# One ordered load queue for a spectral and MLP block: loads moved to SP in a fixed sequence, the output fill behind the last filter load, a new instruction order

## The chip, the core and the metric

The kernel runs on one core of a Trainium2 chip. Times are device microseconds of one launch; smaller is better. The kernel before took 172.88 us as the median of three runs (172.51 to 174.43).

The engines are named as the profile names them: PE (TensorE, matrix products), DVE (VectorE), ACT (ScalarE), POOL (GpSimd) and SP (SyncE, which here only issues DMAs). Names with q are an engine's own queue of issues (SPq, POOLq).

## The reference

With x of 2048 rows and 640 columns, bf16:

```python
xn = _layernorm(x, axis=-1)
return x + _A_ref(xn, A_w_r, A_w_i) + _B_ref(xn, B_w1, B_b1, B_w2, B_b2)
```

`_A_ref` is a 2-D real Fourier transform over rows and columns, a pointwise product with the complex filter `w_r + 1j * w_i` (2048 x 321), and the inverse transform. `_B_ref` is a two-layer perceptron, 640 to 1536 to 640, with the tanh form of gelu between the layers.

## The kernel before

The 2048 rows are cut into 16 chunks of 128; chunk c holds the rows p * 16 + c. Everything stays in on-chip memory between the stages.

- **Normalization and folding (DVE, lines 482 to 542).** Each chunk of x gives statistics (L482, L484), a reciprocal root on POOL (`rstd`, L492), and the normalized chunk `xn` (L510). Chunks go in eight pairs; a pair's columns are folded twice (L538, `xe`; L542, `xf`). `xn` has two slots (`p_xn`), so the third pair has to wait until all readers of the first are done.
- **Transposes of xn.** The perceptron needs `xn` with columns on the partitions (`xnT`). Chunks 0 to 5 are transposed on PE (`tps`, L526) and copied out by ACT or DVE; chunks 6 to 15 (`BYDMA`) by a DMA transpose that SP issues (L517), which reads the `xn` slot.
- **First layer (`hps`).** Row blocks hps0 to hps5 cover chunks 0, 1, 2-3, 4-7, 8-11 and 12-15. Each has 12 column tiles of five matmuls, and ACT applies gelu to each tile (L576, `gT`). hps3 needs xnT4 to xnT7, hps4 needs xnT8 to xnT11.
- **Second layer.** For eight chunks (`KEEP`: 1, 2, 4, 5, 7, 8, 10, 11) it is done early (`kps`, four parts of six matmuls) and DVE puts the sum with b2 aside (L736). It needs W2. For the others it stands at the end (`fps`).
- **Transform.** `aps` is the first transform over rows (table G), one per pair, copied into `XV`; `bps` is the transform over columns (table E), which needs all eight pairs; `cps` finishes the rows (table M); DVE multiplies with the filter (L643, needs every filter load) and adds (L647); `dps` (table N) starts the way back; its results `U` go through 16 DMA transposes (L668) into `XV`; `eps` (table GE) and the last product with table H inside `fps` finish it.
- **Output.** Four DMAs first copy x into the output (`B_pre`, L465, the fill); 14 chunks are then added onto it by accumulating DMAs from POOL (L752), each waiting for its part of the fill; chunks 14 and 15 (`DIRECT`) already hold x and are stored from SP (L749).

All matmuls are recorded on one line (L379) and all loads on one (L374); tiles tell them apart. In the profile `W` stands for W1 or W2 and `X`, `gtab`, `T`, `Wf` for the buffers of that name.

The order is written by hand. Operations are numbered as the program creates them; `ORDER` lists number, engine letter (s SP, p PE, a ACT, d DVE, g POOL) and slots, and each engine runs its own entries in that sequence. Waits are worked out from it. Before the change the loads of x, W1, G, the identity and the filter are on SP; W2 (four pieces), b2 and the tables E, M, N, GE, H are on POOL, as is the fill, which waits for nothing. SP's order before begins x0, x1, a filter load, W1 first part, identity, x2, x4, b1, two filter loads, W1 third part, x6, W1 second part; it goes on with x14, G, x10 and x12 among filter loads; then xnT6 and xnT7, thirteen filter loads, xnT11, xnT10, a filter load, x8 (chunks 8 and 9), and the other transposes among filter loads.

The filter comes in 34 loads of up to 80 KB, made of rows of 642 bytes:

```python
load(bass.AP(tensor=Wf, offset=p0 * WP + off, ap=[[2 * WP, 16], [2 * KP, n], [1, 321]]),
     bass.AP(tensor=wsrc.tensor, offset=wsrc.offset + row * 321, ap=[[128 * 321, 16], [step * 321, n], [1, 321]]),
     B_w, 16 * 642 * n, after=[wpad], rate=250e3, issue=0.645, group="W", prio=next(pr))
```

Of the kernel before, what the change touches and what calls it, by code (L numbers as in the profile page):

```python
# [13 lines left out]
D = 640  # L14
F = 1536
# [263 lines left out]


# [16 lines left out]
def bass_parallel_sum__spectral_gfnet__dense_activation_gelu__prompt_kernel(  # L297
# [12 lines left out]
    const = {k: nc.inline_tensor(_bf16_bits(v.reshape(128, -1)), name=f"c_{k}").ap().bitcast(BF) for k, v in T.items()}  # L310
    xv = A_x[0].rearrange("(p c) d -> p c d", c=16)
    ov = out[0].rearrange("(p c) d -> p c d", c=16)
    w1v = B_w1.rearrange("(c p) f -> p c f", p=128)
    w2v = B_w2.rearrange("(c p) e -> p c e", p=128)
    b1v = B_b1.rearrange("(c p) -> c p", p=128)
    b2v = B_b2.rearrange("(o e) -> o e", o=1)

    K = Sched(nc, ["sp", "pe", "act", "dve", "pool"])
    with ExitStack() as es:
# [29 lines left out]
        W2 = sb("W2", [128, NFC, D])  # L349
# [20 lines left out]
        p_xn, p_x1, p_xf, p_xb, p_y, p_t, p_z, p_u = Pool(2), Pool(1), Pool(2), Pool(2), Pool(2), Pool(2), Pool(2), Pool(3)  # L370
        p_yo, p_y2, p_yf, p_os = Pool(2), Pool(1), Pool(2), Pool(8)

        def load(dst, src, buf, nbytes, after=(), reads=(), rate=400e3, q="sp", prio=400, issue=0.45, late=0.0, group=None):
            return K.op([(q, 1.0 if q == "pool" else issue)], prio, lambda e, _: e.dma_start(dst, src), reads=reads, writes=[buf], after=after, dma=(nbytes, rate), late=late, group=group)  # L374
# [38 lines left out]
        B_w = Buf("W")  # L413
# [27 lines left out]
        load(mtab[:], const["M"], B_m, 65536, rate=200e3, q="pool", prio=next(pr2), late=10.0)
        load(ntab[:], const["N"], B_n, 49152, rate=200e3, q="pool", prio=next(pr2), late=10.0)
        load(getab[:], const["GE"], B_ge, 204800, q="pool", prio=next(pr2), late=10.0)
        load(htab[:].rearrange("p a b -> p (a b)"), const["H"], B_h, 524288, q="pool", prio=next(pr2), late=10.0)
# [6 lines left out]
        for ri, wsrc in enumerate((A_w_r, A_w_i)):  # L451
            for pp in range(2):
                for qq in range(2):
                    for lo in range(2):
# [40 lines left out]
        for pair in range(8):  # L495
# [290 lines left out]
```

## Time and profile before

| | |
|---|---|
| Profiled execution, its own time | 174.47 us |
| Span, first to last instruction | 172.7 us |
| Median of the three runs | 172.88 us |
| PE busy | 147.8 us (86%) |
| DVE busy | 111.8 us (65%) |
| ACT busy | 76.0 us (44%) |
| POOL busy | 27.4 us (16%) |
| Mean granted TensorE clock | 0.951 |
| DMA moved | 20.71 MB, mean 120 GB/s |

The page cuts the span into 40 equal slices and gives each engine's busy share in tenths. A line of the stretches gives, after the length, the busy time and the number of instructions of PE, PEld (weight loads, beside PE), DVE, ACT and POOL, then the granted clock, the busy share of the DMA engines, and GB/s. A line of the waits names who waited for whom, the total, how often, and the longest. The chain that ended last and the timelines give start, duration and what ran; an issue on SPq or POOLq is the time that the queue spends on issuing, not the transfer.

### The profile page before, as it was taken

What the parts mean: (1) busy time and instruction counts of PE and PEld (TensorE: products, weight loads), DVE (VectorE), ACT (ScalarE), POOL (GpSimd) and SP (SyncE); (2) the same over time, 40 slices, a digit from 0 to 9 for tenths busy, and PEclk for the clock granted to TensorE, in tenths of its full rate; (3) what the DMA queues carried; (4) which work ended last, traced back from release to release, by engine and by line L of the source; (5) the groups of instructions that cost most, each with busy time, mean ns of one, the idle gap of its engine ahead of it and who ended that gap; (6) DMA issues with size and microseconds to landing.
All of it is one profiled execution on the core that took longest, in us unless ns stands there. A gap on an engine that the chain in (4) does not pass through costs nothing.

```text
span 172.7 us, 4031 instructions
## 1 busy us (share of the span) xinstructions
PE 147.8 (86%) x1702; PEld 90.7 (53%) x1720; DVE 111.8 (65%) x240; ACT 76.0 (44%) x131; POOL 27.4 (16%) x44
## 2 busy tenths in 40 slices
PE   7631989995980099999999999999899999999994
PEld 7531878862630056645445534445455756575563
DVE  2680389998201981279729848888323999998732
ACT  2450677932670046667736786974321322021000
POOL 1610164153000100000000000000000018333520
PEclk9997599999999558999999999999999999999999
DMA  4999999999999550000002500962843036686392
GB/s 113 295 343 305 311 274 254 211 63 237 400 269 213 120 124 9 4 0 4 0 4 45 110 3 4 98 58 60 96 86 70 0 42 71 88 107 80 38 114 78
DMA packets 29705, 20.71 MB, mean 120 GB/s; under 512 B 19160, under 2 KB 27480, under 8 KB 29688
## 3 DMA queue, kind: packets, MB, share of 16 engines
q1 hardware_dynamic: 26264, 12.37, 36.8%
q0 software_dynamic: 3424, 8.10, 21.9%
q8 instruction: 13, 0.21, 0.5%
q14 instruction: 4, 0.03, 0.1%
HBM read 13.58 MB, written 5.24 MB: 109 GB/s over the span
## 4 chain that ended last, share of the span: by engine, by line
PE 53%; DMA 19%; DVE 14%; SPq 8%; issue 3%; ACT 1%; DVEq 0%
PE ps L379 53%; DMA W<-in_B_w_dram 9%; DMA xnT<-T 6%; SPq L517 4%; SPq L374 4%; DMA XV<-U 2%; DVE stats L482 2%; DMA X<-in_A_x_dram 2%; DVE T L510 2%; DVE W L745 2%; DVE Wf L699 2%; DVE Wf L391 1%; DVE Wf L704 1%; DVE T L542 1%; DVE T L538 1%
## 5 line engine op out<-in xcount | busy, mean ns | idle before, releaser
L379 PE MATMUL ps<-xnT,W 128*128 128x512 bf16 (+2 forms) x360 | 63.2, 326 | 9.1 <-DMA W<-in_B_w_dram 6.7
L379 PE MATMUL ps<-W,gT 128*128 128x128 bf16 (+3 forms) x378 | 54.9, 291 | 1.4 <-issue 0.3
L576 ACT ACTIVATE gT<-ps,b1col 128x512 bf16<-128x512 f32 (+2 forms) x72 | 36.9, 546 | 21.8 <-PE ps L379 21.1
L379 PEld LDWEIGHTS ps<-xnT,W 128*128 128x128 bf16 x360 | 30.4, 105 | 30.4 <-issue 10.6
L379 PEld LDWEIGHTS ps<-W,gT 128*128 128x128 bf16 x396 | 30.7, 98 | 23.2 <-issue 0.8
L752 POOL DMA_DIRECT2D out_dram<-W x14 | 12.1, 901 | 94.6 <-DVE W L745 94.6
L482 DVE BATCH_NORM_STATS2 stats<-X 128x6 f32<-128x320 bf16 x32 | 14.1, 479 | 19.8 <-DMA X<-in_A_x_dram 19.8
L390 ACT ACTIVATE XV<-ps 128x1280 bf16<-128x1280 f32 (+1 forms) x8 | 9.5, 1185 | 16.1 <-PE ps L379 16.1
L379 PE MATMUL ps<-gtab,T 128*128 128x128 bf16 x80 | 7.2, 242 | 9.1 <-DVE T L542 9.1
L390 ACT ACTIVATE Wf<-ps 128x960 bf16<-128x960 f32 (+1 forms) x6 | 5.3, 882 | 21.5 <-PE ps L379 21.5
L492 POOL TENSOR_TENSOR rstd<-ve,mhalf 128x2 f32<-128x2 f32 (+1 forms) x8 | 6.0, 759 | 43.5 <-DVE ve L491 43.5
L643 DVE TENSOR_TENSOR T<-Y,Wf 128x1288 bf16<-128x1288 bf16 x16 | 12.7, 823 | 0.0
L379 PEld LDWEIGHTS ps<-gtab,T 128*128 128x128 bf16 x80 | 6.0, 110 | 11.3 <-DVE T L542 9.9
L391 DVE CAST Y<-ps 128x644 bf16<-128x644 f32 x7 | 5.8, 827 | 9.0 <-PE ps L379 9.0
L390 ACT ACTIVATE Xb<-ps 128x960 bf16<-128x960 f32 (+1 forms) x7 | 7.6, 1099 | 5.7 <-PE ps L379 5.7
L542 DVE TENSOR_TENSOR T<-T 128x512 bf16<-128x512 bf16 (+1 forms) x32 | 9.0, 316 | 1.3 <-PE ps L379 1.2
L736 DVE TENSOR_TENSOR X<-ps,b2bc 128x640 f32<-128x640 f32 x7 | 5.7, 820 | 5.5 <-PE ps L379 5.5
L391 DVE CAST Xb<-ps 128x960 bf16<-128x960 f32 (+1 forms) x5 | 5.9, 1174 | 3.6 <-PE ps L379 3.6
L390 ACT ACTIVATE Y<-ps 128x644 bf16<-128x644 f32 x9 | 6.2, 705 | 3.4 <-PE ps L379 3.4
L379 PE MATMUL ps<-getab,XV 32*128 32x160 bf16 (+1 forms) x128 | 7.6, 242 | 0.0
L510 DVE TENSOR_SCALAR T<-X,mv,rstd 128x640 bf16<-128x640 bf16 x16 | 7.0, 456 | 0.7 <-DMA xnT<-T 0.7
L538 DVE TENSOR_TENSOR T<-T 128x640 bf16<-128x640 bf16 x16 | 7.3, 480 | 0.1
(58 smaller groups left out, 131.7 us busy)
## 6 DMA issues: line engine op xcount, KB each, us to landing
out_dram<-in_A_x_dram POOLq DMA_DIRECT2D x4, 640.0 KB, 9.6
X<-in_A_x_dram SPq DMA_DIRECT2D x7, 320.0 KB, 13.1
out_dram<-W POOLq DMA_DIRECT2D x14, 160.0 KB, 3.5
W<-in_B_w_dram POOLq DMA_DIRECT2D x4, 480.0 KB, 9.1
Wf<-in_A_w_r_dram SPq DMA_DIRECT2D x15, 80.2 KB, 8.4
Wf<-in_A_w_i_dram SPq DMA_DIRECT2D x15, 80.2 KB, 8.0
W<-in_B_w_dram SPq DMA_DIRECT2D x1, 800.0 KB, 10.0
W<-in_B_w_dram SPq DMA_DIRECT2D x1, 640.0 KB, 14.8
```

The lines of the kernel that those rows point to most:

```text
L374: return K.op([(q, 1.0 if q == "pool" else issue)], prio, lambda e, _: e.dma_start(dst, src), reads=reads, writes=[buf], after=after, dma= ...
L379: ins = e.matmul(o_, lhsT=lw, rhs=rh, start=st, stop=sp_, skip_group_check=True)
L390: return e.activation(dst(), src(), ACT.Copy, scale=scale)
L391: return e.tensor_copy(dst(), src())
L482: st_ops.append(K.op([("dve", 0.393)], pr, lambda e, _, c=c, h=h: e.bn_stats(stats[:, c, 6 * h:6 * h + 6], view(X, c * D + H2 * h, [[1, H2 ...
L510: o = K.op([("dve", 0.356)], pr, lambda e, _, c=c, n=n, xnv=xnv: e.tensor_scalar(out=xnv(n, 0, [[1, D]]), in0=view(X, c * D, [[1, D]]), sc ...
L517: ring_ops.append(K.op([("sp", 1.28)], 1500, lambda e, _, c=c, n=n, xnv=xnv: e.dma_start_transpose(xnT[:, c, :, :], xnv(n, 0, [[1, D]])), ...
L538: K.op([("dve", 0.39)], pr, lambda e, _, k=k, op=op, xnv=xnv, x1v=x1v: e.tensor_tensor(out=x1v(H2 * k, [[D, 2], [1, H2]]), in0=xnv(0, 0, [ ...
L542: ring_ops.append(K.op([("dve", 0.333 if w == 128 else 0.136)], pr, lambda e, _, op=op, x1v=x1v, xfv=xfv, o_=o_, o0=o0, o1=o1, w=w: e.tens ...
L576: K.op([("act", act_us(128 * nt, 1) + 0.02)], pr + PRIO["gelu"], lambda e, _, c0=c0, nt=nt, fc=fc, hps=hps: e.activation(gT[:, fc, 128 * c ...
L643: filt_ops.append(K.op([("dve", 0.738)], pr, lambda e, _, k=k, Y=Y, TB=TB, pair=pair: e.tensor_tensor(out=view(TT, TB.slot * 8 * KP + k * ...
L752: last.append(K.op([("pool", 0.9)], 450, lambda e, _, c=c, os_=os_: e.dma_start(ov[:, c, :], view(W1, OST + os_.slot * D, [[1, D]]), accum ...
```

## The change

Three things change. First, the ten loads that POOL issued go to SP, and every SP load must follow the SP load created before it (`hard=queued[-1:]`), so the loads are issued in the order of the program text; E and M are now created before b2. Only DMA transposes stand among them. Second, the four DMAs of the fill stay on POOL, but read the filter's buffer and the last transposed chunk (`reads=[B_w, B_xnT[15]]`), so they wait until both are there. Third, `ORDER` is a new one for all engines.

SP's order after it: x0, W1 first part, identity, x1, W1 second part, b1, x2, W1 third part, G, x4, x6, x8, x10, x12, x14, W2 in four pieces, E, M, b2, N, GE, H, fourteen filter loads, xnT6, one filter load, xnT7, thirteen filter loads, xnT12, one, xnT13, one, xnT8, xnT9, xnT10, xnT11, two, xnT15, xnT14, two filter loads, and then the transposes into `XV`.

```diff
+        queued = []
+
         def load(dst, src, buf, nbytes, after=(), reads=(), rate=400e3, q="sp", prio=400, issue=0.45, late=0.0, group=None):
-            return K.op([(q, 1.0 if q == "pool" else issue)], prio, lambda e, _: e.dma_start(dst, src), reads=reads, writes=[buf], after=after, dma=(nbytes, rate), late=late, group=group)
+            o = K.op([(q, 1.0 if q == "pool" else issue)], prio, lambda e, _: e.dma_start(dst, src), reads=reads, writes=[buf], after=after, dma=(nbytes, rate), late=late, group=group,
+                     hard=queued[-1:] if q == "sp" else [])
+            if q == "sp":
+                queued.append(o)
+            return o
...
         for h in range(4):
-            load(W2[:, 3 * h:3 * h + 3, :], w2v[:, 3 * h:3 * h + 3, :], B_w2, F * D // 2, q="pool", prio=next(pr2), late=8.0, group="w2")
-        load(b2bc[:], bass.AP(tensor=b2v.tensor, offset=b2v.offset, ap=[[0, 128], [1, D]]), B_b2b, 163840, q="pool", prio=next(pr2), late=10.0)
-        load(etab[:], const["E"], B_e, 204800, q="pool", prio=next(pr2), late=10.0)
...
+            load(W2[:, 3 * h:3 * h + 3, :], w2v[:, 3 * h:3 * h + 3, :], B_w2, F * D // 2, prio=next(pr), group="w2")
+        load(etab[:], const["E"], B_e, 204800, prio=next(pr))
+        load(mtab[:], const["M"], B_m, 65536, rate=200e3, prio=next(pr))
+        load(b2bc[:], bass.AP(tensor=b2v.tensor, offset=b2v.offset, ap=[[0, 128], [1, D]]), B_b2b, 163840, prio=next(pr))
...
+            load(ov[:, 4 * c:4 * c + 4, :].rearrange("p c d -> p (c d)"), xv[:, 4 * c:4 * c + 4, :].rearrange("p c d -> p (c d)"), B_pre[c], 2 * 4 * D * 256, q="pool", prio=150 - c, reads=[B_w, B_xnT[15]])
```

In PE's new order kps1 and kps2 come whole before hps3, about nine of the twelve tiles of hps3 and aps3 to aps6 come before hps4, and most of hps5 comes after the last `dps` and before the first `eps`. In DVE's new order the pairs 0, 1, 2, 3, 6, 4, 5, 7 follow each other.

More of the change, by code (lines that the diff above doesn't have):

```diff
@@ L253 @@
 ORDER = """
-8s 2a 0d 5g 1d 4g 3g 7p:0 6g 11s 48s 9s 10s 14s 73d 17s 74d 13s 79d 64s 75d 80d 76a 144p:1 77a 78d 34s 81d 140d:0 82d 15s 143p:2 83g 141p:3 18s 142d 145a 146d 12s 260p:4 85d 254p:5
-55s 255p 147p:6 149d:0 71p:7 261p 33s 92d 148a 25g 95d 72a 22s 257p:6 84d 258p 256a 296p:7 16s 26g 88d 297p 262a 293p:5 298a 20s 294p 96d 290p:4 259a 291p 86d 47s 295a 97d 27g 150d
-281p:7 292a 284p:6 87d 285p 51s 282p 275p:5 286a 151d:0 287p:4 24g 288p 283a 21s 276p 89d 317p:6 100d 289a 318p 314p:7 54s 277a 90d 315p 101d 311p:4 319a 312p 91g 278p:5 316a 153d
@@ L257 @@
-60s 279p 320p:6 313a 102d 321p 103d 23g 269p:7 280a 270p 56s 299p:4 322a 161d:1 300p 305p:5 271a 104d 263p:6 38s 301a 264p 28g 306p 158d 272p:7 265a 273p 323p:4 105d 35s 307a 152d
-162p:0 106d 274a 154d 159p:1 93d 107g 163a 52s 324p 302p:5 164d:0 303p 266p:6 31g 325a 160d 308p:7 49s 309p 304a 267p 188d:0 310a 347p:4 63s 190d 268a 338p:5 32g 94d 332p:7 133d
-189s 333p 98d 136d 350p:6 334a 99g 348p 165d 351p 349a 132d 335p:7 29g 191s 336p 352a 176d:1 329p:4 173d 337a 330p 356p:6 30g 167d:1 169d 331a 116d 174p:7 37s 357p 120d 175a 353p:4
@@ L260 @@
-46s 119d 354p 177p:3 358a 117d 42s 344p:7 355a 121d 118d 345p 134d 359p:6 122d 36s 166d 178a 123g 360p 124d 156p:0 346a 61s 128d 339p 361a 341p:4 125d 340a 62s 342p 155p 127d 343a
-326p:7 168d 39s 157a 327p 129d 598p:4 180d:0 66s 732d 599p 44s 328a 126d 179d 65s 171p:0 135d 170p 182d:0 41s 600p 181d 172a 137d 184d 216d:1 43s 601p 138d 214d 139g 57s 183d
-613p:6 130d 218d:0 217s 131g 602d 186p:0 185p 219d 614p 215s 187a 220d:1 221d 389p:4 222d 223d 40s 377p:5 192d:0 193d 19s 378p 227d:0 615p 58s 379a 195d:0 197d 196d 228s 70g 225p:0
@@ L263 @@
-229d 371p:5 194d 232d:0 68g 224p 230s 390p 231d 226a 616p 235d:1 69g 109d 53s 372p 112d 391a 67g 240d:1 198p:0 50s 373a 199p 233d 374p:4 108d 241s 200a 111d 375p 110d 113d 368p:5
-242d 376a 114d 59s 234d 115g 617d 369p 383p:4 243s 370a 203d:0 384p 201d 236d 392p:5 385a 204s 206d:0 205d 237p:0 238p 209d:0 362p:4 239a 207d 202s 208d 363p 210d 245d:0 380p:6
-364a 244d 45s 211p:0 246d:1 212p 247d 381p 248d 213a 249d 386p:7 387p 382a 250p:0 251p 388a 393p 252d 365p:4 253a 366p 394a 473p:0,0 367a 628p:6 474a 475d 395p:5 470p:0,1 396p 471a
@@ L266 @@
-472d 629p 397a 740d 488p:0 440p:4 490a:0 489d:1 461p:5 491p:0 441p 493a 492d 462p 442a 630p 498d:0 463a 495d:1 476p:0,1 499d 413p:4 477a 478d 414p 425p:5 415a 500d:0 501d 512p:0
-494d 404p:4 513a:0 426p 514a:1 497d:1 631p 496d 427a 502p:0 632d 422p:5 503a:2 504d:0 423p 658p:6 424a 659p 443p:5 444p 660p 445a 515p:0 407p:5 516a 517d 408p 519d:0 505p:0 409a
-405p 518d 506a 437p:5 507d 406a 438p 508s 661p 521d:0 439a 522d:1 479p:0,0 511s 662d 523d 419p:4 510s 480a 481d 420p 398p:5 421a 509s 399p 524d:1 525d 482p:0,1 400a 520d 401p:6
@@ L269 @@
-483a 484d 402p 464p:7 403a 536p:0 465p 537a:0 538d:1 446p:6 466a 529p:0 447p 531a:2 530d:1 410p:7 448a 411p 539p:0 412a 458p:4 541d 540a 459p 547d:1 526p:0 460a 449p:5 527d 528a
-431p:4 546d 532s 485p:0,0 543d:0 452p:6 487a 535s 549d:0 548d 453p 486a 542d 432p 534s 450p 433a 545d:1 560p:0 544d 451a 455p:7 562d:1 533s 561a:0 456p 454a 688p:4 457a 563p:0
-416p:6 565a 564d 417p 571d:1 550p:0 418a 428p:7 566d:0 552a:2 429p 551d:0 689p 430a 570d 553p:0 567d 690p 555a 573d:0 554a 691p 558s 572d 569d:1 643p:6 568d 692d 559s 574p:0 644p
@@ L272 @@
-575a:1 557s 645p 673p:4 556s 576a:2 646p 577p:0 647d 674p 578a 579d 675p 580s 676p 582s 434p:6 677d 435p 583s 703p:4 436a 704p 581s 705p 706p 467p:7 707d 584p:0 468p 586a:0 585d
-621p:4 469a 588d:0 606p:0 587d 590d:0 589d 622p 607a:1 608d 603p:6 623p 604d:0 636p:0 609d:0 605g 610d 591p:6 612d:1 638a:0 637d 592p 593p 611d 639d:0 618p:0 633p:2 619d:1 594p
-634d:0 595p 620g 624p 640d 635g 625p 596d:2 666p:0 626d:3 597g 651p:6 641d:0 668a:1 627g 667d 652p 681p:4 642d 669d:0 648p:0 663p:2 649d:4 653p 670d 650g 654p 664d:5 655p 682p
@@ L275 @@
-672d:1 665g 671d 696p:0 656d:6 683p 657g 698a:0 697d 693p:6 684p 700d:0 694d:7 685p 725p:0 686d:4 695g 711p:6 727a:1 726d 687g 718p:4 699d 712p 701d:0 702d 713p 729d:0 714p 728d
-715p 678p:0 716d:1 708p:2 719p 731d:1 717g 730d 720p 679d:0 721p 709d:2 680g 733p:6 710g 722p 734p 723d:3 735p 724g 748p:4 736p 737p 741p:5 738d:5 742p 743p 739s 744p 745p 749p
-746d:6 750p 751p 752p 755p:6 747s 753d 756p 757p 754s 758p 759p 760d 761s
+8s 2a 1d 3g 0d 4g 5g 6g 7p:0 9s 10s 11s 12s 13s 70d 14s 69d 15s 71d 16s 72a 17s 73a 74d 136d:0 18s 76d 137p:1 19s 139p:0 75d 140p:2 20s 141a 138d 77d 21s 257p:4 78d 258p 263p:5 79g
@@ new lines @@
+22s 264p 67p:6 269p:7 23s 68a 270p 81d 24s 266p:6 271a 83d 267p 259a 254p:7 25s 80d 268a 255p 260p:4 265a 261p 26s 142d 272p:6 256a 273p 82d 27s 262a 143p:5 145d:0 274a 28s 275p:4
+146d 144a 276p 281p:7 84d 29s 284p:6 285p 277a 282p 147d:0 299p:5 30s 286a 300p 149d 293p:4 283a 294p 31s 311p:6 150d 301a 85d 312p 296p:7 148d 32s 295a 86d 297p 152p:0 87g 313a
+89d 33s 317p:5 298a 318p 91d 151p 319a 305p:4 34s 154d:1 306p 153a 278p:6 100d 302p:7 155p:5 35s 99d 303p 279p 108d 304a 36s 280a 101d 156d 323p:7 307a 324p 37s 314p:6 157d 315p
@@ new lines @@
+325a 290p:5 291p 115d 316a 158p:4 38s 292a 124d 287p:7 288p 320p:6 39s 159d 321p 289a 308p:5 309p 322a 129d 338p:4 40s 310a 161d:0 356p:7 332p:6 96d 41s 357p 121d 341p:5 42s 358a
+97d 342p 333p 160d 343a 359p:7 43s 98d 360p 334a 163d:1 102d 335p:5 165d 44s 103g 120d 361a 336p 350p:6 104d 337a 45s 351p 122d 184d:0 347p:7 352a 348p 128d 46s 326p:5 349a 164d
+327p 185s 186d 353p:6 328a 354p 116d 344p:7 88d 355a 345p 339p 117d 47s 90d 346a 329p:5 92d 330p 340a 112d 187s 598p:6 331a 732d 613p:4 107d 48s 93d 109d 614p 94d 113d 95g 49s 123d
@@ new lines @@
+615p 114d 50s 172d:1 118d 169d 51s 119g 599p 125d 130d 126d 162d 52s 127g 170p:3 132d 166p:0 53s 175d:0 171a 167p 105d 600p 54s 168a 176d 106d 601p 55s 180d:0 110d 178d 111g 179d
+56s 177d 173p:3 602d 616p 174a 57s 225d:1 181p:0 58s 189d:0 389p:6 617d 59s 390p 60s 182p 223d 391a 395p:7 188d 224s 131d 183a 380p:4 192d:1 133d 392p:5 191d 197d:0 61s 134d 190d
+396p 135g 193d 226s 199d 377p:6 397a 227d:0 378p 228d 194p:0 62s 230d:0 379a 368p:7 232d 231d 198s 229d 195p 371p:6 201d:0 196a 202d 372p 212d:1 200s 393p 203d:1 373a 210d 233p:0
@@ new lines @@
+234p 205d 394a 374p:6 211s 206d 204d 235a 214d:0 375p 215d 362p:5 213s 219d:0 218d 376a 208p:0 216d 207p 217d 363p 236d:0 209a 63s 238d 365p:6 241d:0 64s 366p 240d 364a 220p:0 239s
+221p 244d:1 367a 404p:5 245d 242d 222a 243d 431p:6 237s 432p 246p:0 433a 405p 65s 247p 406a 66s 401p:6 249d 248a 402p 398p:5 403a 470p:0,0 422p:6 471a 472d 252g 423p 473p:0,1 250g
+424a 253g 410p:6 474a 475d 411p 251g 399p 412a 488p:0 400a 369p 489d:0 490a:1 407p:6 370a 428p:5 491p:0 425p:7 493a 492d 426p 498d:0 476p:0,0 427a 499d 416p:7 494d:1 478a 417p 477d
@@ new lines @@
+408p 418a 429p 409a 500d:0 381p 501d 515p:0 430a 495d 643p:6 382a 516d:1 517a:0 644p 497d:1 512p:0 496d 419p:5 513a 514d 420p 519d:0 502p:0 421a 455p:4 522d:1 504a:2 456p 523d
+503a:0 452p:5 518d 457a 453p 505p:0 454a 413p:4 506d 507a 386p:5 524d:0 508s 387p 520d:1 521d 479p:0,0 388a 525d 510s 383p:5 480a 481d 511s 384p 414p 385a 740d 482p:0,1 415a 509s
+645p 483a 484d 646p 539p:0 647d 673p:4 541a:0 540d:1 674p 536p:0 675p 537a 538d 676p 542d:0 546d:1 526p:0 628p:6 527a:2 677d 528a:1 629p 547d 529p:0 543d 703p:4 530a 549d:0 544d:1
@@ new lines @@
+531a 704p 532s 545d 548d 485p:0,0 535s 705p 486a 487d 706p 534s 560p:0 707d 630p 533s 562a:0 561d:1 631p 563p:0 632d 658p:4 565a 564d 659p 571d:0 550p:0 570d 660p 551a:2 566d:1
+552a:0 661p 567d 553p:0 662d 688p:6 554a 568d:0 555a 689p 573d:1 557s 572d 690p 569d 559s 691p 574p:0 692d 558s 458p:4 576a:1 459p 556s 464p:5 460a 465p 437p:4 575a:0 438p 466a
+577p:0 439a 440p:6 578d 579a 441p 581s 434p:7 442a 443p:5 582s 444p 446p:4 445a 447p 583s 435p 448a 449p:6 436a 580s 467p:5 468p 450p 469a 461p:7 451a 462p 584p:0 463a 591p:4
@@ new lines @@
+586a:0 585d 592p 587d:0 588d 636p:0 590d:0 589d 593p 637a:1 638d 594p 640d:0 595p 639d 603p:6 606p:0 596d:0 642d:1 597g 651p:4 607a:0 641d 652p 604d:1 608a 653p 605g 609d:0 663p:6
+610d 648p:0 654p 664d:2 655p 611d:0 665g 711p:6 649d:3 712p 612d 650g 713p 656d:4 618p:2 657g 633p:4 619d:5 714p 634d:6 620g 696p:0 635g 621p:4 698a:1 697d 622p 699d:0 623p 700d
+624p 702d:1 701d 625p 666p:0 626d:7 627g 715p 668a:0 667d 681p:4 682p 716d:0 683p 670d:0 717g 669d 733p:6 672d:0 708p:0 671d 684p 709d:1 685p 693p:2 686d:2 710g 678p:0 734p 694d:3
@@ L278 @@
+687g 718p:4 679d:0 695g 719p 680g 725p:0 720p 727a:1 726d 721p 729d:0 728d 722p 730d:0 735p 723d:4 736p 731d 724g 748p:4 749p 741p:5 737p 742p 738d:5 743p 744p 739s 745p 755p:6
+746d:6 756p 750p 751p 747s 752p 757p 753d 758p 759p 754s 760d 761s
 """
@@ L435, in bass_parallel_sum__spectral_gfnet__dense_activation_gelu__prompt_kernel @@
             load_x(c, 2, next(pr))
-        pr2 = iter(range(300, 200, -1))
         for h in range(4):
-            load(W2[:, 3 * h:3 * h + 3, :], w2v[:, 3 * h:3 * h + 3, :], B_w2, F * D // 2, q="pool", prio=next(pr2), late=8.0, group="w2")
-        load(b2bc[:], bass.AP(tensor=b2v.tensor, offset=b2v.offset, ap=[[0, 128], [1, D]]), B_b2b, 163840, q="pool", prio=next(pr2), late=10.0)
-        load(etab[:], const["E"], B_e, 204800, q="pool", prio=next(pr2), late=10.0)
[L441 to L444, printed above, removed]
+            load(W2[:, 3 * h:3 * h + 3, :], w2v[:, 3 * h:3 * h + 3, :], B_w2, F * D // 2, prio=next(pr), group="w2")
+        load(etab[:], const["E"], B_e, 204800, prio=next(pr))
+        load(mtab[:], const["M"], B_m, 65536, rate=200e3, prio=next(pr))
+        load(b2bc[:], bass.AP(tensor=b2v.tensor, offset=b2v.offset, ap=[[0, 128], [1, D]]), B_b2b, 163840, prio=next(pr))
+        load(ntab[:], const["N"], B_n, 49152, rate=200e3, prio=next(pr))
+        load(getab[:], const["GE"], B_ge, 204800, prio=next(pr))
+        load(htab[:].rearrange("p a b -> p (a b)"), const["H"], B_h, 524288, prio=next(pr))
         WP = 32 * KP
@@ L462, in bass_parallel_sum__spectral_gfnet__dense_activation_gelu__prompt_kernel @@
                             load_w(wsrc, p0 + 1, off + 2 * KP, 127, 7, -1)
-        B_pre = [Buf(f"pre{c}") for c in range(4)]
-        for c in range(4):
-            load(ov[:, 4 * c:4 * c + 4, :].rearrange("p c d -> p (c d)"), xv[:, 4 * c:4 * c + 4, :].rearrange("p c d -> p (c d)"), B_pre[c], 2 * 4 * D * 256, q="pool", prio=150 - c, late=32.0)
         B_b1ps, B_b1c = Buf("b1ps", psum), Buf("b1col")
@@ L557, in bass_parallel_sum__spectral_gfnet__dense_activation_gelu__prompt_kernel @@
                      reads=[aps], writes=[B_xa[pair]])
+        B_pre = [Buf(f"pre{c}") for c in range(4)]
+        for c in range(4):
+            load(ov[:, 4 * c:4 * c + 4, :].rearrange("p c d -> p (c d)"), xv[:, 4 * c:4 * c + 4, :].rearrange("p c d -> p (c d)"), B_pre[c], 2 * 4 * D * 256, q="pool", prio=150 - c, reads=[B_w, B_xnT[15]])
         B_gT = {}
```

## The prediction

> **What bounds the kernel now.** I read the page's slices first, then busy time by stretch, then who waited for whom, then the chain that ended last and the timelines of the two queues that issue DMAs.
>
> ```profile
> PE   7631989995980099999999999999899999999994
> PEclk9997599999999558999999999999999999999999
> DMA  4999999999999550000002500962843036686392
> GB/s 113 295 343 305 311 274 254 211 63 237 400 269 213 120 124 9 4 0 4 0 4 45 110 3 4 98 58 60 96 86 70 0 42 71 88 107 80 38 114 78
> ```
>
> A slice is 4.32 us. From slice 14 (60 us) PE is full to the end; before it PE has holes while the DMA engines are full. So the first 60 us belong to the loads, the other 112 us to TensorE.
>
> ```profile
> 6.00:41.20 35.20, 24.88 (x275) 20.91 (x278) 25.07 (x81) 19.16 (x46) 13.73 (x21) 0.90 1.10 249
> 41.20:51.30 10.10, 10.03 (x65) 5.11 (x65) 3.06 (x9) 6.15 (x8) 0.00 (x0) 1.00 1.19 343
> 51.30:60.40 9.10, 0.04 (x1) 0.04 (x2) 4.83 (x16) 0.01 (x1) 0.71 (x1) 0.75 0.71 160
> 60.40:71.00 10.60, 10.50 (x76) 6.30 (x78) 4.53 (x14) 6.33 (x9) 0.00 (x0) 0.73 0.25 56
> 71.00:172.70 101.70, 97.54 (x1234) 53.67 (x1248) 71.76 (x111) 41.67 (x67) 12.12 (x14) 1.00 0.38 53
> ```
>
> The first column after the stretch is its length, the second PE busy, the third from the end the granted clock. 51.3 to 60.4 is a pure hole. After it the clock is 0.50 until 66.0, so 5.6 us there do 2.8 us of work. From 71.0 PE idles only 4.16 us, the tail included.
>
> ```profile
> DVE stats L482 <- DMA X<-in_A_x_dram: 19.8, 3, 9.9
> PE ps L379 <- DVE T L542: 9.1, 1, 9.1
> PE ps L379 <- DMA W<-in_B_w_dram: 6.7, 2, 5.7
> ```
>
> ```profile
> 31.16 9.95 DMA xnT<-T
> ...
> 43.99 4.01 SPq L517
> 48.00 0.04 issue
> 48.04 3.23 SPq L517
> ...
> 51.95 3.56 DMA X<-in_A_x_dram
> ...
> 60.36 10.54 PE ps L379 x76
> ```
>
> The hole waits for DVE, DVE for the load x8 (chunks 8 and 9), and x8 for SP, which sat 7.2 us in the issues of xnT11 and xnT10 ahead of it.
>
> ```profile
> 25.64 8.29 SPq L517 DMA_TRANSPOSE xnT<-T  x2
> 53.24 2.60 SPq L517 DMA_TRANSPOSE xnT<-T  x2
> 38.11 2.11 POOL L374 DMA_DIRECT2D out_dram<-in_A_x_dram  x4
> ```
>
> The first two transposes cost SP 8.3 us while POOL's tables were in flight, the next two 8.1 us while the fill was (38.1 to its landing at 51.4), later ones 1.3 us each.
>
> **The change, part by part.** The base is the profiled span, 172.7 us.
>
> (1) Ten loads (W2 four times, b2, E, M, N, GE, H) leave POOL, which loses 4 x 0.83 + 6 x 0.6 = 6.9 us of issuing; POOL is 16% busy, so that is worth nothing. SP gains 10 issues of 0.45 to 0.6 us, 5.5 us. The DMA engines hide them: at 9 to 16 us one SP issue already takes 1.4 to 1.9 us, so SP waits for the DMAs. Uncovered they would cost the 5.5 us.
>
> (2) The fixed order puts x0, W1, x1..x15, W2 and the tables first, then 34 filter loads. Bytes ahead of the first filter load: x 2.62 MB, W1 1.97, G 0.52, I 0.03, W2 1.97, tables 1.21, together 8.33 MB. Slices 1 to 6 mean 297 GB/s, so 28.0 us; the first packet moves at 2 us (x0 lands at 3.13), so 30.0. x14 then lands near 19 and x8 near 16 instead of 55.5: **the wait that makes the hole is gone**. W1's last part lands near 12 (before: 22.3), W2 near 26. Fourteen filter loads come before xnT6. Their 642-byte packets ran 304 in the us from 40.0, 0.42 us for one load of 128: 12.6 full ones, 5.3 us, 35.3. xnT6, one filter load and xnT7 have 640 + 128 + 640 packets; at 640 to 700 packets per us (transposes at 52 and 63 us) 2.4 us, and 1.4 us to complete: **xnT7 lands at 39.1** (before 41.1). With every later transpose at its 1.28 us SP is free of xnT7 at about 35.4.
>
> (3) SP behind it, with 0.64 us per filter load (0.60 and the gap) and 1.32 per transpose: 13 filter loads, 43.7; xnT12, filter load, xnT13, filter load, 47.6; xnT8 and xnT9, 50.3; xnT10 and xnT11, 52.9. Landing is 2.6 us after issue, so xnT11 is there at 54.3. DVE must keep pace: it is fed from x14 on, and from the copy of xnT3 (20.4, after the tps3 matmuls) its list to xn_8 is 22.6 us of rows (L482 0.48, L510 0.45, L538 0.47, L542 0.41 and 0.2, L736 0.82), so 43.0, and to xn_11 4.8 more, 47.8. xn_11 also needs the slot that xnT12 and xnT13 read (48.4). xn_10 then ends at 49.8, before SP wants it. **hps4, the block on chunks 8 to 11, can start at 54.3; I take 55**, between 50.4 (when PE could reach it, below) and 71.2 (a rival).
>
> (4) PE until then. hps0 and hps1 go at ACT's 0.37 us per L576 from 12 us; hps2 from 20.4, 12 x 0.6, to 27.6; W2 is there at 26. Five parts of kps at 0.82 reach 31.7, xn_4 comes at 33.4, aps1, three parts of kps and half of aps2 end at 38.0. hps3 can start at 39.1. From there to hps4 the order holds 9.2 rows of hps3 at 1.08 and 4.5 aps at 0.56: 12.4 us. So PE idles 1.2 us before xnT7 and about 3.5 before hps4, too short to lose the clock to go by the 1.8 us idle at 39.4, after which it stayed 1.00; at worst 2.8 us, as above.
>
> (5) The fill now waits on POOL for the last filter load and xnT15. Behind it stand only the 14 output accumulations; all rstd come ahead. The last filter load is issued at 58.1 and lands at 60.6; the fill took 13.3 us, so 74. The first accumulation stood at 138, now near 126: 50 us of cover, cost nothing. What is won is in (2): no fill beside transposes. The filter multiply L643 that needs all filter loads started at 77.8; here its place comes near 67, 6 us after the landing.
>
> (6) The new order of the rest. The same instructions; eps0 follows all of kps and hps. I take the 4.16 us of waits that the stretch from 71.0 has, and 0.5 more for aps7, whose xf7 DVE finishes at 56.8. The trace shows none of this order: bounds 0 and +8.
>
> **Sum.** Work left when xnT7 lands, at full clock: 10.03 + 10.50 - 2.8 + 97.54 = 115.3; two parts of kps2 more, less half an aps, are already done (2 x 0.82 - 0.28): 113.9. Minus 12.4: 101.5 left at hps4. 55 + 101.5 + 4.2 + 0.5 = **161.2 us span**, 11.5 less. The profiled execution took 174.47, 1.77 over its span, and 1.59 over the median of the runs; so 161.2 + 1.77 - 1.59 = 161.4 us as a median.
>
> **Rivals.**
>
> The transposes stay slow in pairs (0.17). For: xnT6 and xnT7 took SP 8.29 us instead of 2.6 and landed 14.3 and 10.0 us after issue, and two instruction packets (queue q8) passed between 33 and 52 us, as they may again. Against: both slow pairs had POOL's traffic beside them, now gone. Price 5.7 us, once: 166.9.
>
> TensorE alone is the bound (0.13): DMA and SP run ahead, as when a transpose costs SP no more than the 0.39 to 0.42 us of a 160 KB X load; six of them 5.3 us less. Then PE reaches hps4 at 38.0 + 12.4 = 50.4, or DVE allows it at 52: 156.5 to 158. Against it stand ten transposes, none under 1.28 us. [...]
>
> **Slower (0.10): one queue throttles SP.** A transpose among filter loads costs SP what the four in a loaded queue did: 5.47, 2.77, 4.83, 3.23, mean 4.07 us. For: all filter loads are now in that queue. Against: 53.24 shows two at 1.28 us right behind a filter load and x8. Then SP from 35.4: 15 filter loads and six transposes, 9.6 + 24.4, and a landing 1.8 later: hps4 at 71.2. PE idles nearly 20 us and loses 2.8 to the clock: 71.2 + 101.5 + 4.7 + 2.8 = 180. It is slower than before once hps4 passes 55 + 11.5 = 66.5, so from 1.32 + 11.5 / 6 = 3.2 us per transpose.
>
> The change doesn't bring what it frees (0.05): the hole goes, and the rewritten order waits as long after 71. For: one chain cps, L643, dps, XV, eps must fit under hps5; against: 101.7 us with 4.16 idle. Time about 172, both signs.
>
> **How the numbers follow.** Forecast 0.55, TensorE-bound 0.13, slow pairs 0.17, lost later 0.05, slower 0.10. The first three span 156.5 to 167, with the bounds of (6) on top 169: range 156 to 169, leaving out 0.15. A measurement of this kernel tells about 1%, 1.7 us, from no change. Faster 0.55 + 0.13 + 0.17 + 0.02 = 0.87, same 0.03, slower 0.10.
>
> **What would show it.** Right: the 9.9 us wait of L482 for X gone; xnT7 near 39; transposes after it at 1.3 us on SP; hps4 near 55; no clock of 0.5 after 20 us; the fill at 61 on POOL. Wrong: L517 issues of 3.2 us or more beside filter loads, PE waiting for xnT over 10 us, or a new hole after 71 us in front of L643 or eps.

## The result, and the profile after

The kernel after takes 160.28 us, the median of four runs (159.53 to 160.96), against 172.69 us for the kernel before measured beside it. The ratio is 0.9264, with a 95% interval of 0.9184 to 0.9344: 7.4% faster. The profiled execution took 159.53 us, 1.83 over its span of 157.7. Forecast were 161.4 us and a span of 161.2.

The slices of the page of the kernel after, one of 3.94 us each:

```profile
PE   7879899967998799999999999999999999999993
PEclk9968999996999999999999999999999999999999
DMA  4999999998455537910062025044440079834953
GB/s 116 313 389 399 364 360 260 169 126 152 96 128 132 125 83 209 386 78 4 4 123 44 4 56 119 0 87 84 83 87 0 0 87 94 114 42 50 130 69 88
```

The two slices without PE are gone. Counted from 0, the full load stretch ends with slice 8 (35 us); slices 2 to 5 run at 360 to 399 GB/s, where slices 1 to 6 of before had 254 to 343. The fill is the 386 GB/s in slice 16 (63 to 67 us), behind every load. The granted clock is below full in two places, slices 2 to 3 and 9.

The same kernel's busy time in three stretches, cut at the starts of hps3 and hps4. The columns are the stretch, its length, and busy time with instructions of PE, PEld, DVE, ACT and POOL, then granted clock, DMA share and GB/s:

```profile
0.00:36.58 36.58, 30.73 (x334) 25.81 (x337) 29.27 (x95) 20.18 (x46) 5.61 (x15) 0.95 1.04 276
36.58:52.72 16.14, 14.45 (x92) 7.46 (x93) 9.80 (x33) 10.43 (x13) 0.93 (x1) 0.89 0.54 119
52.72:157.70 104.98, 101.01 (x1278) 56.23 (x1293) 70.70 (x109) 46.88 (x79) 14.52 (x18) 1.00 0.43 83
```

PE idles 5.85 + 1.69 = 7.5 us before hps4 starts and 3.97 after it. In the kernel before it idled 20.7 us up to 71.0 (1.2 of them in the first 6 us) and 4.16 behind. So 13.2 of the 15.0 us of span are idle time taken out of the load phase; nearly nothing came from the long rest.

Who waited for whom, after (total, times, longest), and the chain that ended last where it enters hps4:

```profile
DVE T L511 <- DMA xnT<-T: 5.6, 1, 5.6
DVE stats L483 <- DMA X<-in_A_x_dram: 5.6, 4, 2.4
...
PE ps L385 <- DMA xnT<-T: 3.6, 2, 2.5
```

```profile
44.24 2.66 DMA xnT<-T
...
50.17 2.45 DMA xnT<-T
52.72 17.34 PE ps L385 x224
```

The statistics no longer wait 9.9 us for one load. Line numbers moved by one to six: L517 of before is L518, L510 is L511, L379 is L385. What the chain now runs through is SP's row of transposes, one every 1.32 us: xnT11 lands at 52.62 and hps4 starts at 52.72. Between the two landings shown it passes through DVE, which had nothing to do until xnT13 landed at 46.90 and freed the `xn` slot of the next pair:

```profile
46.93 0.45 DVE L511 TENSOR_SCALAR T<-X,mv,rstd 128x640 bf16<-128x640 bf16 x1 [5.59 <-DMA xnT<-T]
```

### The profile page after: what moved, and what is told of

Same layout as the page of the kernel before. It is cut to its first block, busy times and chain, and to the rows that moved or that the text cites. A ratio compares the mean times of both kernels' runs of the same rounds, so it can differ in the third digit from the quotient of the medians.

```text
span 157.7 us, 4031 instructions
## 1 busy us (share of the span) xinstructions
PE 146.2 (93%) x1703; PEld 89.5 (57%) x1720; DVE 109.8 (70%) x234; ACT 77.5 (49%) x137; POOL 21.1 (13%) x34
## 4 chain that ended last, share of the span: by engine, by line
PE 69%; DVE 10%; SPq 9%; DMA 7%; issue 2%; ACT 1%
PE ps L385 69%; SPq L376 7%; DVE stats L483 4%; DMA W<-in_B_w_dram 4%; DMA xnT<-T 3%; SPq L518 2%; DVE T L539 1%; DVE T L543 1%; DVE T L511 1%; ACT XV L396 1%; DVE mv L485 1%; PE ps L527 1%; DVE xnT L719 1%; ACT gT L581 0%; DVE xnT L397 0%
## 5 line engine op out<-in xcount | busy, mean ns | idle before, releaser
L385 PE MATMUL ps<-xnT,W 128*128 128x512 bf16 (+2 forms) x360 | 60.0, 320 | 5.7 <-DMA xnT<-T 3.6
L385 PE MATMUL ps<-W,gT 128*128 128x128 bf16 (+3 forms) x382 | 54.8, 292 | 1.5 <-issue 1.1
L385 PEld LDWEIGHTS ps<-xnT,W 128*128 128x128 bf16 x360 | 30.4, 102 | 27.2 <-issue 5.8
L581 ACT ACTIVATE gT<-ps,b1col 128x512 bf16<-128x512 f32 (+2 forms) x72 | 36.3, 547 | 16.5 <-PE ps L385 15.5
L385 PEld LDWEIGHTS ps<-W,gT 128*128 128x128 bf16 x396 | 29.8, 98 | 22.6 <-issue 2.2
L396 ACT ACTIVATE Wf<-ps 128x960 bf16<-128x960 f32 (+1 forms) x7 | 6.2, 893 | 24.3 <-PE ps L385 24.3
L397 DVE CAST Wf<-ps 128x960 bf16<-128x960 f32 (+1 forms) x5 | 5.1, 1024 | 10.8 <-PE ps L385 10.8
L648 DVE TENSOR_TENSOR T<-Y,Wf 128x1288 bf16<-128x1288 bf16 x16 | 12.3, 822 | 0.0
L511 DVE TENSOR_SCALAR T<-X,mv,rstd 128x640 bf16<-128x640 bf16 x16 | 6.9, 435 | 5.6 <-DMA xnT<-T 5.6
L397 DVE CAST Xb<-ps 128x960 bf16<-128x960 f32 (+1 forms) x6 | 6.7, 1124 | 5.0 <-PE ps L385 5.0
L396 ACT ACTIVATE Y<-ps 128x644 bf16<-128x644 f32 x8 | 5.7, 708 | 6.9 <-PE ps L385 6.9
L397 DVE CAST Y<-ps 128x644 bf16<-128x644 f32 x8 | 6.6, 823 | 3.5 <-PE ps L385 3.4
L396 ACT ACTIVATE Xb<-ps 128x960 bf16<-128x960 f32 (+1 forms) x6 | 6.8, 1139 | 3.7 <-PE ps L385 3.7
L385 PE MATMUL ps<-getab,XV 32*128 32x160 bf16 (+1 forms) x128 | 7.6, 242 | 0.0
L385 PEld LDWEIGHTS ps<-getab,XV 32*128 32x128 bf16 (+1 forms) x128 | 6.4, 147 | 1.6 <-DMA XV<-gtab 0.4
```

Source lines behind the costliest of these rows:

```text
L385: ins = e.matmul(o_, lhsT=lw, rhs=rh, start=st, stop=sp_, skip_group_check=True)
L396: return e.activation(dst(), src(), ACT.Copy, scale=scale)
L397: return e.tensor_copy(dst(), src())
L511: o = K.op([("dve", 0.356)], pr, lambda e, _, c=c, n=n, xnv=xnv: e.tensor_scalar(out=xnv(n, 0, [[1, D]]), in0=view(X, c * D, [[1, D]]), sc ...
L581: K.op([("act", act_us(128 * nt, 1) + 0.02)], pr + PRIO["gelu"], lambda e, _, c0=c0, nt=nt, fc=fc, hps=hps: e.activation(gT[:, fc, 128 * c ...
L648: filt_ops.append(K.op([("dve", 0.738)], pr, lambda e, _, k=k, Y=Y, TB=TB, pair=pair: e.tensor_tensor(out=view(TT, TB.slot * 8 * KP + k * ...
```

## The experiments

The predicted mechanism had three parts that the diff mixes: loads no longer on POOL, a late fill, a new order. All experiments ran beside the kernel before (172.81 and 172.82 us); the kernel after was timed beside another set of it (172.69 us), so a difference of a few microseconds from the kernel after is less sure than one from the kernel before.

**x8 alone.** The prediction read the hole at 51 us as a wait for x8. The kernel before, with only that load issued early, from right behind x14:

```diff
-... 192d:0 193d 19s 378p ...
+... 72a 22s 19s 257p:6 ...
```

> The kernel before, with one load moved: x8 goes right behind x14 on SP instead of behind xnT11 and xnT10. Theory A (the late load x8 makes PE's hole at 51 to 60 us, as the chain of waits says): the hole of 9.1 us nearly goes and the half clock behind it too, 172.7 becomes 162 us. Theory B (the slow transposes make the hole; x8 only stands behind them): DVE passes the statistics of chunk 8 at once, but xn_14 then waits for the slot that xnT11 and xnT10 read, which land at 53.2 and 53.9; DVE resumes at 54 instead of 55.5 and the hole shrinks by 2 us at most: 170 to 171 us.

Measured: 172.19 us, ratio 0.998 (0.9951 to 1.0009). x8 lands at 34.38 instead of 55.5, and the hole stays, 6.91 us of PE. DVE's timeline (start, duration, instruction, in brackets the idle before it and its releaser):

```profile
55.01 0.45 DVE L510 TENSOR_SCALAR T<-X,mv,rstd 128x640 bf16<-128x640 bf16 x1 [7.06 <-DMA xnT<-T]
```

DVE now waits 7.06 us to write `xn`, whose slot xnT11 and xnT10 still read; they land at 54.32 and 54.98. x8 came last in the chain and was not the cause by itself: the two transposes ahead of it in SP's queue also hold the slot that DVE writes next. Theory B named this wait; its 170 to 171 us did not come, and the two transposes landed 1.1 us later than it assumed. A chain names the wait that ended last, and another one of nearly the same length can lie under it.

**The fill alone.** The kernel before, with the fill waiting for the last filter load and xnT15 on POOL:

```diff
+        for o in fill:
+            o.deps += B_w.writers + B_xnT[15].writers
```

> The kernel before, with the fill alone changed: it waits for the last filter load and xnT15, all else as it was. Theory B (the fill's traffic is what makes xnT11 and xnT10 cost SP 4.8 and 3.2 us): they cost 1.3 us each, x8 is issued near 46.5 and lands near 49, DVE resumes 6.3 us earlier, the hole shrinks to 3 us and the clock stays up: 172.7 - 6.3 - 2.8 = 163.6 us. Rival (a transpose behind filter loads in its own queue is slow, whatever POOL does): the two still cost 3 to 5 us, no change beyond 1 us, 172 us.

Measured: 170.66 us, ratio 0.9862 (0.9784 to 0.994), 2.1 us less: a gain, but whether it reaches 2% is unclear. SP's timeline:

```profile
44.01 3.67 SPq L518 DMA_TRANSPOSE xnT<-T  x2
```

The two issues that took 8.1 us beside the fill take 3.67, and xnT11 and xnT10 land 3.56 and 2.49 us after their issue instead of 10.06 and 5.82. So the fill did slow them, though xnT11 still took 2.35 us of SP instead of 1.28. The expected time missed because SP reached xnT11 no earlier than before: it stands behind thirteen filter loads, and ahead of those xnT6 and xnT7 still cost 7.27 us beside POOL's tables. x8 lands at 52.27 and 5.74 us of the hole are left.

**The fill early again.** The kernel after, with `reads` taken off the fill and its four issues moved up in POOL's order:

```diff
-B_pre[c], 2 * 4 * D * 256, q="pool", prio=150 - c, reads=[B_w, B_xnT[15]])
+B_pre[c], 2 * 4 * D * 256, q="pool", prio=150 - c)
...
-... 472d 252g 423p 473p:0,1 250g 424a 253g ... 251g ...
+... 396p 135g 252g 250g 253g 251g 193d ...
```

> The changed kernel, with the fill waiting for nothing: POOL issues it behind the last rstd, near 33 us, so that it runs beside xnT7, the filter loads and xnT12. If the fill slows transposes: the ones issued while it runs cost SP 3 to 5 us, hps4 starts 5 to 10 us later than 52.7, 160.3 becomes 166 to 170 us. Rival (it only shares bandwidth, and SP's issue rate sets the pace there, not the DMA engines): hps4 moves by 2 us or less, 160 to 162.5 us.

Measured: 166.25 us, ratio 0.9625 (0.9585 to 0.9665): 6.0 us above the kernel after. Its waits:

```profile
DVE T L511 <- DMA xnT<-T: 11.8, 1, 11.8
...
PE ps L385 <- DVE T L543: 7.9, 1, 7.9
```

The fill, issued at 38.0 to 40.3, lands at 43.5 to 49.9. Beside it xnT12, xnT13 and xnT8 take SP 1.59, 2.52 and 2.46 us, less than the 3 to 5 expected, and xnT12 lands at 51.30, 9.2 us after its issue (45.06 and 2.79 in the kernel after). The filter loads issued at 38.55 to 41.5 also land 8 to 10 us after their issue: the whole of SP's queue was slow, not transposes alone. DVE and then PE wait for it, and hps4 starts at 59.26, 6.54 us later. This is the hole of the kernel before, made again by one edit.

**The ten loads on POOL again.** The kernel after, with W2, the tables and b2 in POOL's queue:

```diff
-load(W2[:, 3 * h:3 * h + 3, :], w2v[:, 3 * h:3 * h + 3, :], B_w2, F * D // 2, prio=next(pr), group="w2")
+load(W2[:, 3 * h:3 * h + 3, :], w2v[:, 3 * h:3 * h + 3, :], B_w2, F * D // 2, q="pool", prio=next(pr), group="w2")
... (E, M, b2, N, GE, H alike)
```

> The changed kernel, with the ten loads (W2, E, M, b2, N, GE, H) back on POOL at their places in the order, all else as in the change. Theory (the step from POOL to SP is itself worth nothing, as step 1 of the prediction has it): 160.3 us within 1.5. Rival (one queue is what makes the early loads fast: beside POOL's packets W1, G and x arrive later, and tables in flight slow xnT6 and xnT7): first layer and hps3 later by 3 to 6 us, 163 to 166 us.

Measured: 163.03 us, ratio 0.9388 (0.9313 to 0.9464), 2.7 us above the kernel after. The intervals of the two ratios overlap, the times do not (161.51 to 164.17 against 159.53 to 160.96). Its waits, and where PE starts hps3:

```profile
DVE stats L483 <- DMA X<-in_A_x_dram: 15.0, 9, 2.7
```

```profile
42.96 1.24 PE L385 MATMUL ps<-xnT,W 128*128 128x512 bf16 x5
```

The ten loads now move beside x: x8 lands at 20.3 instead of 15.8 and x14 at 28.5 instead of 18.4. DVE waits 15.0 us for x instead of 5.6, hps3 starts at 42.96 instead of 36.58, hps4 at 55.41. The transposes take 1.28 to 1.42 us of SP. So the queue of POOL costs here by bringing W2 and the tables beside x. The rival's other half, that tables in flight slow xnT6 and xnT7, is not tested: the last table landed at 29.9 and xnT6 was issued at 32.72.

**The old order.** The kernel after in loads and fill, with the order of before on PE, ACT, DVE and POOL. SP's loads keep the sequence of after; the transposes stand in the places of after, but follow each other as before (xnT11 and xnT10 ahead of xnT12), because DVE makes `xn` in that order. PE's line is L379 there, as before. The edit in words:

```diff
-ORDER: p, a, d and g entries in the sequence of the kernel after
+ORDER: p, a, d and g entries in the sequence of the kernel before (the places of s entries and the late fill as after)
```

> The order of PE, ACT, DVE and POOL's own work as before the change; SP's loads, the ten loads on SP, and the late fill as after it (SP: the loads in the fixed order, fourteen filter loads, xnT6, one, xnT7, thirteen, xnT11, xnT10, one, xnT12, one, xnT13, two, xnT14, xnT15, xnT9, xnT8, two). Theory (the loads and the fill make the gain, the new order of the rest adds little): xnT7 lands near 36.5, PE has 115.3 us of work from there and waits some 3 us for hps5's transposes and aps7 besides the usual 4: span 159, median about 161 us. Rival (the new order of PE and DVE is what uses the early loads): PE still has a hole of 5 us or more before aps or hps5, median 166 us or more.

Measured: 165.08 us, ratio 0.9506 (0.9433 to 0.9578), 4.8 us above the kernel after. DVE's timeline, then PE's:

```profile
46.02 0.45 DVE L511 TENSOR_SCALAR T<-X,mv,rstd 128x640 bf16<-128x640 bf16 x1 [4.54 <-DMA xnT<-T]
```

```profile
51.24 1.04 PE L379 MATMUL ps<-gtab,T 128*128 128x128 bf16 x8 [5.02 <-DVE T L543]
```

hps3 starts at 36.19, as early as in the kernel after. But the old order then asks for `xn` whose slot waits for xnT10 and xnT11 (landed 44.94 and 46.00), PE has nothing else in its order and stands 5.02 us, and the clock is 0.50 from 49.76 to 56.59. The forecast of 161 missed, the rival nearly hit: the new order, that of the transposes included, is worth 4.8 us, since it gives PE and DVE work between the transposes.

**The transposes earlier.** If SP's row of transposes sets hps4, then filter loads ahead of it can give way: the filter's first use, L648, starts at 65.68. The kernel after with SP's entries in another sequence, in words:

```diff
-14 filter loads, xnT6, 1, xnT7, 13, xnT12, 1, xnT13, 1, xnT8, xnT9, xnT10, xnT11, 2, xnT15, xnT14, 2
+8 filter loads, xnT6, xnT7, 11, xnT12, xnT13, xnT8, xnT9, xnT10, xnT11, 10, xnT15, xnT14, 5
```

> The changed kernel with SP's order alone edited: xnT6 and xnT7 come after eight filter loads instead of fourteen and fifteen, then eleven filter loads, xnT12, 13, 8, 9, 10, 11 in one go, ten filter loads, xnT15, xnT14 and the last five. Theory (after the loads are in, PE waits only for transposes that stand behind filter loads: 2.5 us at hps3, 0.6 at aps and 1.1 at hps4): these waits go, hps3 starts at 34.1 and hps4 at 48.6 instead of 52.7; span about 154, median 156 us. Rival (DVE's own list sets aps and so hps4, the transposes only look late): xn_8 to xf7 still takes until 55, gain 1 us or less, 159 us or more.

Measured: **155.22 us** (153.57 to 155.51), ratio 0.8975 (0.8912 to 0.9039), faster than both kernels; 5.1 us below the kernel after. PE's timeline:

```profile
33.44 1.24 PE L385 MATMUL ps<-xnT,W 128*128 128x512 bf16 x5 [0.35 <-DMA xnT<-T]
...
47.31 1.89 PE L385 MATMUL ps<-xnT,W 128*128 128x512 bf16 x8 [0.62 <-ACT gT L581]
```

hps3 starts 3.14 us earlier and hps4 5.41 earlier, at waits of 0.35 and 0.62 us, the second no longer for a transfer. From hps4 on it takes 106.4 us, 1.4 more than the kernel after. The last filter load lands at 61.52 instead of 58.49, and the multiply L648 waits 1.2 us for the filter. The granted clock is 1.00 throughout in the profiled execution. One thing is not explained: xnT7 took SP 3.38 us there (issued at 26.52, landed at 33.19), although POOL's queue moved nothing then (its first transfer, the fill, waits for the filter load that landed at 61.52); table H, in SP's own queue, landed only at 29.67. So this transpose was slow to issue without POOL's queue at work.

Put in a row by medians: before 172.7; fill late 170.7; loads on SP in the fixed sequence too 165.1; the new order, that of the transposes included, too 160.3; transposes earlier 155.2. Undone from the kernel after, the fill costs 6.0, the loads' queue 2.7 and the order 4.8. These overlap: their sum is 13.5 where all together gave 12.4, and the fill's price is 2.1 or 6.0 by what else has been mended.

## Why the prediction was right, and where its steps were not

**Right in kind.** The hole went, xnT6 and xnT7 took SP 1.31 and 1.28 us and later ones 1.28, the fill on POOL cost nothing (issued 58.80, landed 68.98 for the 74 given), and no rival came about: no transpose among filter loads took over 1.31 us, and nothing waits long behind 71 us (PE's longest wait there is 0.16 us). The span of 157.7 does lie in the 156.5 to 158 of the rival "TensorE alone", so the time alone can't tell them apart; the waits can: hps4 still waited 1.11 us for xnT11, and a transpose cost SP 1.28 us, not 0.4. Slow transposes are not ruled out in general: moved earlier in the last experiment, one took SP 3.38 us.

**Step (1), POOL to SP "worth nothing", was mis-sized.** Counting issue time only, it missed what x shares the DMA engines with: beside the ten loads x14 landed at 28.5 instead of 18.4, and the kernel took 2.7 us more. Step (2) had part of it, with x14 put near 19 (18.37) and x8 near 16 (15.82).

**Step (2), the rate.** 297 GB/s came from slices in which filter loads stood among x and W1; without them 360 to 399 were reached. W2 landed at 23.8, not 26, and xnT7 at 36.33, not 39.1. The sentence that the early x8 takes the hole away failed as a cause: alone it is worth nothing, and xnT11's slot held the hole up as well.

**Step (3), SP's pace.** 0.64 per filter load and 1.32 per transpose held; shifted by the earlier xnT7, xnT12 was issued at 42.27 (43.7), xnT11 landed at 52.62 (54.3), hps4 started at 52.72 (55). The DVE sum was too long: it put xn_8's work at 43.0, yet DVE wrote xn_8 at 36.67, was through with its pair at 41.34 and then waited 5.59 us for xnT13 (landed 46.90, 48.4 given). In the trace of the kernel after, consecutive DVE rows start closer together than their listed durations (0.40 us apart where a row says 0.48, at 30 us).

**Step (4), PE.** PE was ready for hps3 at 34.1 (38.0), waited 2.49 us (1.2 expected), then 0.57 and 1.11. "Too short to lose the clock" was wrong: after the 2.49 us the clock was 0.50 for 3.41 us, which cost 1.7 us of work, and the sign "no clock of 0.5 after 20 us" failed with it. By this count it cost the end nothing, but only because hps4 waited for xnT11 anyhow; without it PE would have waited some 2.8 us there instead of 1.11. The work between hps3 and hps4 was sized right: 14.45 us busy, less those 1.7, is 12.7 where 12.4 were counted.

**Step (6), the rest.** 101.01 us of PE busy against 101.5, and 3.97 us idle against 4.7.

**The sum** of span missed by 3.5 us: 2.3 from hps4 and 1.2 from the rest. In medians only 1.1 of it shows, since this profiled execution lies 0.75 below its median, while before's lay 1.59 above. That closeness is luck.

## What to carry to other kernels

Transfers that something waits for should not share the DMA engines with a bulk copy that nothing waits for, even in another queue: give the copy a wait that puts it behind them. Here the shared stretch cost 2.1 us in one kernel and 6.0 in the other. When a chain blames one late load, ask what would be waited for if it were early; one run with only that load moved answers it. And once a queue sets the pace, reorder inside it by first use: here moving seven filter loads behind xnT7 and eleven behind xnT11 brought another 5.1 us without touching another engine.

## What the runs showed of the hardware that was not expected

**Beside the fill, SP's queue moved as many packets and an eighth of the bytes.** The DMA part of the kernel before, 42 to 49 us, with the fill in q0 (POOL) and filter loads in q1 (SP): packets, MB, share of the engines' time.

```profile
q0 software_dynamic: 532, 2.48, 86.1%
q1 hardware_dynamic: 536, 0.31, 15.4%
```

The two moved 532 and 536 packets, but 2.48 MB for the fill and 0.31 for SP's queue, whose rows have 642 bytes and less: 44 GB/s over the 7 us. Alone it ran at 195 GB/s in the us from 40.0 (336 packets, none in q0). The early fill in the third experiment gave 481 and 415 packets from 40 to 47 us. The counts are not near each other everywhere: the same run had 448 and 811 from 42 to 49 us, and the fourth, with W2 and tables in q0 beside x in q1, had 401 and 1403 from 8 to 20 us (1.81 and 2.73 MB). So no run here shows by what rule the two queues share the DMA engines.

**The stretches at half clock came in steps of 3.41 us.** In all eight profiled executions every stretch at 0.50 inside the span lasted a multiple of 3.41 us (3.41, 6.83, 10.24, once 13.65), and within an execution they start a whole number of 3.41 us apart (9.44 and 36.75 in the kernel after). Two answers for steps of that length, first of the kernel after, up to and from the 36.75 at which its clock fell, then of the one with the early fill, counted back from the 48.90 at which its clock fell:

```profile
33.34:36.75 3.41, 0.92 (x10) 0.58 (x9) 3.41 (x11) 0.39 (x1) 0.00 (x0) 1.00 1.03 163
36.75:40.16 3.41, 3.41 (x13) 1.60 (x12) 2.83 (x12) 1.38 (x2) 0.93 (x1) 0.50 0.49 98
```

```profile
31.83:35.25 3.42, 1.99 (x21) 1.22 (x19) 3.42 (x10) 1.00 (x2) 0.93 (x1) 1.00 1.32 128
35.25:38.66 3.41, 2.26 (x15) 1.22 (x16) 3.38 (x12) 0.98 (x2) 1.57 (x2) 1.00 0.65 127
```

The idle of 2.49 us fell whole into one such step, PE was busy 0.92 us of it, and the next ran at 0.50. The idle of 2.58 us in the other kernel fell into two, with 1.99 and 2.26 us busy, and the clock stayed at 1.00. So an idle of about 2.5 us cost 1.7 us in one execution and nothing in the other. That it goes by where the idle falls is the author's estimate from these two; no run here shows what sets the steps or their start.
